# Two items' last k-times-v chunks in one 64x64 step of the array, and the pair stretch moved ahead of the second product

## The chip, the cores and the metric

The kernel runs on one core of a Trainium2 chip. The metric is device time in microseconds (us), lower is better, as the median of several executions. Engines: TensorE (PE, its weight loads PEld), VectorE (DVE), ScalarE (ACT), GpSimd (POOL), SyncE (SP, which issues most transfers).

## The reference

```python
def _attn_ref(q, k, v):               # (8, 8, 576, 64) each, float32
    q_s = softmax(q, axis=-1)         # written out: max, exp, sum + 1e-9, divide
    k_s = softmax(k, axis=2)          # over the 576 rows
    kv = np.einsum('bhsd,bhse->bhde', k_s, v)
    return np.einsum('bhsd,bhde->bhse', q_s, kv)

def _moe_ref(x, w_in, w_out):         # x: (4608, 512), 512 -> 2048 -> 512
    h = x @ w_in
    g = h * np.tanh(softplus(h))      # Mish
    return g @ w_out
```

The attention's output, heads side by side, is `x`.

## The kernel before

The 64 (batch, head) pairs are worked as 32 items of two heads each, four items to a block of 512 columns of x. Everything is float32; a matmul of plain float32 shows in the trace as two records, one for each of two passes. The MLP's factors are split into a high and a low part (`xs`, `wih`/`wil`, `gh`/`gl`, `wo`), three matmuls for each product.

The MLP runs in 144 slots (`NSLOT`). Slot n has a first product `h_mm(n)` (12 matmuls of 128x128 weights by 512 columns into one bank `ph`), Mish on ACT (`g_mish`, tile `y`), the split on DVE (`g_hi`, `g_lo`), and three slots later a second product `out_mm` (12 matmuls into four banks `po`). The order of the start is written out by hand in `FIRST`; after it `group(n)` takes four slots at a time, u = 0 to 3, with i = 4 + n/4 the number of the item whose attention is spread over that group. In a group, `m` is the slot of the first product and `o = m - 3` that of the second.

At u = 2 of every second group (i = 8, then i = 9, 11 to 31) stands `a_pair(e)`: for items e and e+1 the product of q and kv, namely `px` (512 columns, banks e and f) and `pt` (the last 64 columns), and for items f = e+2 and e+3 the product of k and v into `pkv` (`a_kv2`). Pair 6 (at i = 8) has only the k-times-v part, pair 30 only the px and pt part; pairs 8 to 28 have both.

k times v contracts the 576 rows in five chunks: four of 128 rows, and a last one of 64 real rows, with v's other 64 rows zero. Each chunk is two matmuls, one for each half of the output's partitions (128 rows by 64 columns of weights, `128*64` in the trace). px and pt use quarters of the array (`64*64`), four at a time.

After the matmuls, `a_tail2` (ACT) copies pt, `x_hi` (ACT) and `x_lo` (DVE) split px into `xs`, and `a_kvs2` (DVE) divides the k-times-v product by its sum into `kvt`, which the next pair's px and pt read. `pt`, `pkv` and the first product's `ph` share two banks g and h, taken in turn by `turn_bank`. At the end `evac` copies the last four `po` banks out; for the last of them ACT copies one half and DVE the other.

Of the kernel before, what the change touches and what calls it, by code (L numbers as in the profile page):

```python
# [9 lines left out]
F32 = mybir.dt.float32  # L10
F32R = mybir.dt.float32r
U32 = mybir.dt.uint32
AF = mybir.ActivationFunctionType
ALU = mybir.AluOpType
AX = mybir.AxisListType
P = 128
# [37 lines left out]
def attn_mish_mlp(ctx: ExitStack, tc: tile.TileContext, q, k, v, wu, qs, kt, v3, out):  # L54
# [32 lines left out]
    def bank(letter, name, dtype=F32):  # L87
        return ps.tile([P, 512], dtype, tag=f"bank_{letter}", name=name)
# [4 lines left out]
    def turn_bank(name):  # L93
        turn.append("gh"["gh".index(turn[-1]) ^ 1] if turn else "g")
        return bank(turn[-1], name)
# [78 lines left out]

    at = {}
    xs = {}
    ap.tile([P, 104], F32, tag="gap0", name="gap0")
    xt_dram = dp.tile([B, P, HP, ST], F32, name="xt_dram")


# [1 line left out]
    def v_tile(pool, tag, inner=False):  # L182
        if inner:
            t = pool.tile([P, D + 2, 2, NC + 1], F32, tag=tag, name=f"{tag}_0")
            ones, last = t[:, D:D + 2], t[ST:P, D:D + 2, :, NC]
        else:
            t = pool.tile([P, 2, NC + 1, D + 2], F32, tag=tag, name=f"{tag}_0")
            ones, last = t[:, :, :, D:D + 2], t[ST:P, :, NC, D:D + 2]
        nc.gpsimd.memset(ones, 1.0)
        nc.gpsimd.memset(last, 0.0)  # L190
        return t
# [36 lines left out]
    def v_load(i):  # L228
        if i >= NITEM:
            return  # L230
        t = at.setdefault(i, {})["v"] = pools["v"] if i > HP and i % 2 else vt[min(i, 3)]
        if i < 3:
            nc.sync.dma_start(t[:, 0:D], v3[i])
        else:
            nc.sync.dma_start(t[:, :, :, 0:D], v[i])

    def v_part(i, j, c):
        t = at[i]["v"]
        return t[:, :, j, c] if i < 3 else t[:, j, c]
# [170 lines left out]
    def a_x2(e, px, pt, order):  # L410
        for x, j, h in order:
            a, o = slice(h * D, (h + 1) * D), slice((h ^ j) * D, ((h ^ j) + 1) * D)
            nc.tensor.matmul((px, pt)[x][h][o], kvt[a, j], at[e + j]["qT"][x][a], start=True, stop=True)  # L413
        for j in range(2):
            at[e + j].update(dict(px=px[j]) if px else {}, **dict(pxt=pt[j]) if pt else {})
# [8 lines left out]
        fill(f"XP{e}", px[0])  # L424
        a_x2(e, px, None, [(0, j, h) for j in range(2) for h in range(2)])

    def a_xpair(e):
        r1, r2 = (turn_bank(f"pt{e}_{j}") for j in range(2))
        px = [bank("ef"[j], f"px{e + j}") for j in range(2)]
        a_x2(e, px, (r1[:, 0:ST], r2[:, 2 * (D + 2):2 * (D + 2) + ST]),  # L430
             [(x, j, h) for x in (1, 0) for j in range(2) for h in range(2)])
        return r2

    def a_kv2(e, pkv):
        for i in range(e, e + 2):
            f = slice((i - e) * (D + 2), (i - e + 1) * (D + 2))
            for c in range(NC + 1):
                for j in range(2):
                    nc.tensor.matmul(pkv[j * D:(j + 1) * D, f], at[i]["ke"][:, c, j], v_part(i, j, c),  # L439
                                     start=c == 0, stop=c == NC)  # L440
        at[e]["pkv"] = pkv[:, 0:2 * (D + 2)].rearrange("p (i f) -> p i f", i=2)

    def a_kvp(e, b):
        pkv = bank(b, f"pkv{e}")
        fill(f"KP{e}", pkv)
        a_kv2(e, pkv)

    def a_kvs2(e):
        pkv = at[e]["pkv"]
        rs = ap.tile([P, 2], F32, tag="rs0", name=f"rs{e}")  # L450
        nc.vector.tensor_scalar_add(rs, pkv[:, :, D], 1e-9)
        nc.vector.reciprocal(rs, rs)
        nc.vector.tensor_tensor(kvt, pkv[:, :, 0:D], rs.unsqueeze(2).to_broadcast([P, 2, D]), ALU.mult)

    def a_pair(e):

        f = e + 2
        r2 = a_xpair(e) if e >= COLS else turn_bank(f"pkv{f}")
        if f < NITEM:
            a_kv2(f, r2)  # L460
        if e >= COLS:
            a_tail2(e)
            a_tail3(e)
            for j in range(2):
                x_hi(e + j, at[e + j]["px"])
                x_lo(e + j, at[e + j]["px"])
            a_tail2(e + 1)
            a_tail3(e + 1)
        if f < NITEM:
            a_kvs2(f)  # L470

# [3 lines left out]
    def a_tail2(i):  # L475
        if i < COLS:
            if not xt_first:
                xt_first.append(xp.tile([P, 16, ST], F32, tag=f"wo{NF - 1}", name="xt_first"))
            xt = xt_first[0][:, i]
        else:  # L480
            xt = ap_odd[:, 1] if i % 2 else ap.tile([P, ST], F32, tag="xt", name=f"xt{i}")
        at[i]["xt"] = xt
        nc.scalar.copy(xt, at[i]["pxt"])

    def a_tail3(i):
        b, hp = divmod(i, HP)
        nc.sync.dma_start(xt_dram[b, :, hp, :], at[i]["xt"])
# [30 lines left out]
    def h_mm(n):  # L518
        for t in range(HP):
            h_part(n, t)  # L520
# [42 lines left out]
            nc.tensor.matmul(po[t], g[a][:, t * P:(t + 1) * P], wo[f][:, z], start=f == 0 and i == 0,  # L563
                             stop=f == NF - 1 and i == 2)

    def evac(c, t, *copies):
        ob = sp.tile([P, DM], F32, tag="wc", name=f"ob{c}_{t}")
        w = DM // len(copies)
        for j, copy in enumerate(copies):
            copy(ob[:, j * w:(j + 1) * w], po[t][:, j * w:(j + 1) * w])  # L570
        if c < COLS // HP:
            nc.sync.dma_start(out[c * S:c * S + SM, :].rearrange("(p c) e -> p c e", c=NC)[:, t, :], ob)
        elif c < B:
            nc.sync.dma_start(out[c * S + t * P:c * S + (t + 1) * P, :], ob)
        else:
            for j, eng in enumerate((nc.sync, nc.scalar)):
                e = (2 * t + j + 1) * S
                eng.dma_start(out[e - ST:e, :], ob[j * ST:(j + 1) * ST])

    def group(n):  # L580
        i = HP + n // G

        ka, kb = (i + 2, NITEM) if i % 2 else (COLS + 1 if i == COLS else NITEM, i + 2)
        for u in range(G):
            m, o = n + u, n + u - LAG
            if m < NSLOT:
                h_mm(m)
            if u == 0:
                if NITEM <= i < NITEM + HP:
                    t_load(i - NITEM)  # L590
                if i == COLS:
                    v_load(i + 1)
                a_qsum(i)
                if i < NITEM:
                    a_qmul(i)
            if u == 1:
                a_qt(i)
                a_ksub(ka)
            if 0 <= o < NSLOT:
                out_mm(o)  # L600
            if m < NSLOT:
                g_mish(m)
            if 0 <= o < NSLOT and o % NF == NF - 1:
                for t in range(NC):
                    evac(o // NF, t, nc.scalar.copy if t % 2 else nc.vector.tensor_copy)
            if m < NSLOT:
                g_hi(m)
                g_lo(m)
            if u == 0:
                a_kmx(ka)  # L610
                if ka < NITEM:
                    kt_load(ka + 1)
            if u == 1:
                a_exp(ka, "k")
                if ka < NITEM:
                    k_load(ka + 1)
                a_qm(i + 1)
            if u == 2:
                if i % 2 and COLS < i < NITEM:
                    a_pair(i - 1)  # L620
                    v_load(i + 3)
                    v_load(i + 4)
                elif i == COLS:
                    a_pair(i - 2)
                    v_load(i + 2)
                    v_load(i + 3)
                elif NITEM <= i < NITEM + HP:
                    x_hi(i, tails[i - NITEM])
                    x_lo(i, tails[i - NITEM])
                a_kmx(kb)  # L630
                if kb < NITEM:
                    kt_load(kb + 1)
            if u == 3:
                a_ksub(kb)
        a_exp(kb, "k")
        a_exp(i + 1, "q")
        if kb < NITEM:
            k_load(kb + 1)
        q_load(i + 2)
# [16 lines left out]
    with tc.manual_schedule(engines={ET.Activation, ET.PE, ET.DVE, ET.Pool, ET.SP}):  # L656
        for token in first:
            name, number, banks = re.fullmatch("([A-Z]+)([0-9]*)([a-h]*)", token).groups()
            stages[name](*([int(number)] if number else []), *([banks] if banks else []))
            if name == "H" and banks in ("g", "h"):  # L660
                turn[:] = [banks]
        for n in range(NF, NSLOT, G):
            group(n)

        for t in range(NC):
            for n in range(NSLOT - LAG, NSLOT):
                out_part(n, t)
            evac(B, t, nc.scalar.copy, *([nc.vector.tensor_copy] if t == NC - 1 else []))


# [43 lines left out]
```

## Time and profile before

| | |
|---|---|
| median of 3 runs | 867.15 us (867.15 to 868.44) |
| profiled execution, its own time | 867.23 us |
| its span, first to last instruction | 865.4 us (1.83 us lie around it) |
| mean granted TensorE clock | 0.998 |
| PE busy | 850.8 us (98%) |
| DVE, ACT, POOL busy | 459.1, 327.9, 142.5 us |

PE is busy nearly throughout and its granted clock is full, so the time is the number of PE instructions by their spacing, plus what is lost between unlike ones. Start times of successive matmuls say more than the busy time, since the records overlap.

### The profile page before, as it was taken

To read this page: it belongs to the slowest core of one execution; us is meant where nothing else is said; L and a number is where in the kernel's file an instruction comes from. 1 tells how busy PE (TensorE), PEld (TensorE's weight loads), DVE (VectorE), ACT (ScalarE), POOL (GpSimd) and SP (SyncE) were. 2 spreads that over 40 slices of the span, in tenths; PEclk is the share of its full clock that TensorE was granted. 3 is DMA by queue.
4 is the path that set the end of the run, shared out by engine and by line. 5 is a ranking of instruction groups with operands and counts; after the bars stand their busy time and mean duration, and the time that the engine had idled before them with its cause. 6 is when DMAs were issued, how large, how long until landed. Compare 5 with 4: busy or idle time off the path is not lost.

```text
span 865.4 us, 11716 instructions
## 1 busy us (share of the span) xinstructions
PE 850.8 (98%) x4468; PEld 689.5 (80%) x4468; DVE 459.1 (53%) x1207; ACT 327.9 (38%) x485; POOL 142.5 (16%) x128
## 2 busy tenths in 40 slices
PE   7899999999999999999999999999999999999997
PEld 6677878787878888787878787878788788888886
DVE  6888876646574647464655656564743222222221
ACT  4889854424342434333342334243422111111111
POOL 8996520011111110011111011111110000000000
PEclk9999999999999999999999999999999999999999
DMA  9975335203222223212231313122100020001001
GB/s 332 357 290 144 113 86 151 66 25 83 80 65 46 73 48 120 49 57 63 91 77 44 77 63 91 29 62 83 54 16 0 16 73 13 0 1 49 1 0 49
DMA packets 69944, 67.87 MB, mean 78 GB/s; under 512 B 49024, under 2 KB 49024, under 8 KB 69888
## 3 DMA queue, kind: packets, MB, share of 16 engines
q1 hardware_dynamic: 69568, 66.60, 26.0%
q8 instruction: 35, 0.57, 0.3%
q10 hardware_dynamic: 320, 0.52, 0.2%
q14 instruction: 21, 0.17, 0.1%
HBM read 56.62 MB, written 10.49 MB: 78 GB/s over the span
## 4 chain that ended last, share of the span: by engine, by line
PE 91%; ACT 2%; DVE 2%; POOL 2%; DMA 2%; issue 1%; POOLq 0%; ACTq 0%; DVEq 0%; SPq 0%
PE ph L515 43%; PE po L563 43%; PE pt L439 2%; PE px L413 1%; DMA raw_out<-in_w_dram 1%; PE pkv L439 1%; POOL kt L313 1%; ACT wa L131 0%; PE pt L413 0%; POOL q L370 0%; DMA q<-in_q_dram 0%; ACT ph L534 0%; ACT L534 0%; POOL q L112 0%; DMA xt_dram<-xt_first 0%
## 5 line engine op out<-in xcount | busy, mean ns | idle before, releaser
L515 PE MATMUL ph<-xs,wih 128*128 128x512 f32 x1152 | 358.4, 392 | 1.1 <-DVE gl L112 1.1
L563 PE MATMUL po<-wo,gh 128*128 128x512 f32 x1152 | 355.2, 389 | 1.2 <-POOL wo L112 1.2
L563 PEld LDWEIGHTS po<-wo,gh 128*128 128x128 f32 x1152 | 216.1, 188 | 47.2 <-POOL wo L112 1.6
L515 PEld LDWEIGHTS ph<-xs,wih 128*128 128x128 f32 x1152 | 213.7, 188 | 49.4 <-issue 1.6
L515 PE MATMUL ph<-xs,wil 128*128 128x512 f32 x576 | 224.6, 390 | 0.0
L563 PE MATMUL po<-wo,gl 128*128 128x512 f32 x576 | 224.1, 389 | 0.0
L538 ACT ACTIVATE y<-ph 128x512 f32<-128x512 f32 x128 | 76.7, 599 | 373.5 <-PE ph L515 314.0
L543 DVE CAST gh<-y 128x512 fp32r<-128x512 f32 x128 | 57.4, 449 | 271.5 <-ACT y L538 271.3
L515 PEld LDWEIGHTS ph<-xs,wil 128*128 128x128 f32 x576 | 108.1, 188 | 23.4 <-POOL wil L112 0.4
L563 PEld LDWEIGHTS po<-wo,gl 128*128 128x128 f32 x576 | 108.1, 188 | 22.6
L112 DVE TENSOR_TENSOR gl<-y,gh 128x512 fp32r<-128x512 f32 x128 | 88.6, 692 | 11.9
L370 POOL TENSOR_TENSOR qe<-qe,qs 128x576 f32<-128x576 f32 x24 | 27.9, 1163 | 296.5 <-DVE qs L366 296.5
L538 ACT ACT_TABLE_LOAD x35 | 44.9, 1283 | 71.3 <-PE ph L515 71.3
L112 POOL TENSOR_TENSOR q<-q,qm 128x576 f32<-128x576 f32 (+1 forms) x32 | 38.1, 1193 | 197.8 <-DVE qm L267 186.6
L347 ACT ACT_TABLE_LOAD x43 | 55.2, 1283 | 6.1 <-DMA q<-in_q_dram 3.7
L570 DVE COPY ob<-po 128x512 f32<-128x512 f32 (+1 forms) x17 | 11.5, 676 | 38.5 <-PE po L563 29.1
L356 DVE TENSOR_REDUCE qs<-qe 128x18 f32<-128x576 f32 x24 | 18.1, 752 | 25.2 <-ACT qe L347 25.2
L495 DVE TENSOR_TENSOR xs<-px,xs 128x512 fp32r<-128x512 f32 x32 | 20.7, 685 | 17.0 <-ACT xs L492 16.8
L276 DVE TENSOR_REDUCE qm<-q 128x18 f32<-128x576 f32 (+1 forms) x32 | 24.4, 762 | 4.3 <-DMA q<-in_q_dram 4.2
L246 DVE TENSOR_REDUCE mxd<-kt 128x1 f32<-128x576 f32 x32 | 23.8, 745 | 1.5 <-DMA kt<-in_kt_dram 1.5
L252 DVE STREAM_TRANSPOSE mb<-mxd 32x32 f32<-32x32 f32 x96 | 19.5, 203 | 3.1
L492 ACT CAST xs<-px 128x512 fp32r<-128x512 f32 x32 | 17.4, 591 | 7.4 <-PE px L413 7.4
(115 smaller groups left out, 566.5 us busy)
## 6 DMA issues: line engine op xcount, KB each, us to landing
kt<-in_kt_dram SPq DMA_DIRECT2D x32, 288.0 KB, 2.9
k<-in_k_dram SPq DMA_DIRECT2D x27, 320.0 KB, 3.0
raw_in<-in_w_dram SPq DMA_DIRECT2D x16, 512.0 KB, 7.9
raw_out<-in_w_dram SPq DMA_DIRECT2D x16, 512.0 KB, 5.6
out_dram<-ob SPq DMA_DIRECT2D x32, 256.0 KB, 2.2
q<-in_qs_dram SPq DMA_DIRECT2D x24, 288.0 KB, 3.0
v<-in_v_dram SPq DMA_DIRECT2D x18, 320.0 KB, 3.8
v_odd<-in_v_dram SPq DMA_DIRECT2D x14, 320.0 KB, 4.6
```

Source lines behind the costliest of these rows:

```text
L112: eng.tensor_tensor(out, a, b, ALU.subtract)
L246: nc.vector.tensor_reduce(mxd, r["kt"], axis=AX.X, op=ALU.max)
L252: nc.vector.transpose(mb[h, h], mxd[h].to_broadcast([32, 32]))
L276: nc.vector.tensor_reduce(qm, qt, axis=AX.X, op=ALU.max)
L347: nc.scalar.activation(e, r[nm], AF.Exp)
L370: eng.tensor_tensor(q2, q2, z.unsqueeze(2).to_broadcast(list(q2.shape)), ALU.mult)
L439: nc.tensor.matmul(pkv[j * D:(j + 1) * D, f], at[i]["ke"][:, c, j], v_part(i, j, c), start=c == 0, stop=c == NC)
L495: nc.vector.tensor_tensor(xs[i][:, 1], src, xs[i][:, 0].bitcast(F32), ALU.subtract)
L515: nc.tensor.matmul(gs[n], wi[a][:, t, fs], x[:, z], start=t == 0 and i == 0, stop=t == HP - 1 and i == 2)
L538: nc.scalar.activation(y, gs[n], AF.Mish)
L543: copy(hi, gs[n])
L563: nc.tensor.matmul(po[t], g[a][:, t * P:(t + 1) * P], wo[f][:, z], start=f == 0 and i == 0, stop=f == NF - 1 and i == 2)
```

## The change

In a pair the order on PE becomes: px, pt, four chunks of item f, four chunks of item f+1, and then the two last chunks together as four matmuls of 64 rows by 64 columns, each on a quarter of the array: item f in rows 0 to 63, item f+1 in rows 64 to 127. For that the host rolls the tail rows of v of items 5, 7, ... by 64 and `v_tile` clears the other half of `v_odd`. The two items of a pair write to two banks, each shared with one of the pt tiles: `r[0]` and `r[1]` instead of `r2` alone.

The whole pair (PE, ACT and DVE parts) now stands between `h_mm(m)` and `out_mm(o)` of u = 2, with `g_mish(m)` ahead of it, and so `g_hi(m)` and `g_lo(m)` behind it. At u = 1 of those groups a Mish of one column (`early`) is added behind the exp of k. `a_kvs2` reads two banks (five DVE instructions in place of three). The last `evac` is one copy on ACT.

```diff
-            ones, last = t[:, :, :, D:D + 2], t[ST:P, :, NC, D:D + 2]
+            ones = t[:, :, :, D:D + 2]
+            last = t[0:ST, :, NC, D:D + 2] if tag == "v_odd" else t[ST:P, :, NC, D:D + 2]
...
-    def a_xpair(e):
-        r1, r2 = (turn_bank(f"pt{e}_{j}") for j in range(2))
-        px = [bank("ef"[j], f"px{e + j}") for j in range(2)]
-        a_x2(e, px, (r1[:, 0:ST], r2[:, 2 * (D + 2):2 * (D + 2) + ST]),
-             [(x, j, h) for x in (1, 0) for j in range(2) for h in range(2)])
-        return r2
...
+    def a_kvi(pkv, i, last=NC + 1):
+        for c in range(last):
+            for j in range(2):
+                nc.tensor.matmul(pkv[j * D:(j + 1) * D], at[i]["ke"][:, c, j], v_part(i, j, c),
+                                 start=c == 0, stop=c == NC)
...
+        for i in range(2):
+            nc.vector.tensor_scalar_add(rs[:, i:i + 1], pkv[i][:, D:D + 1], 1e-9)
         nc.vector.reciprocal(rs, rs)
-        nc.vector.tensor_tensor(kvt, pkv[:, :, 0:D], rs.unsqueeze(2).to_broadcast([P, 2, D]), ALU.mult)
+        for i in range(2):
+            nc.vector.tensor_tensor(kvt[:, i], pkv[i][:, 0:D], rs[:, i:i + 1].to_broadcast([P, D]), ALU.mult)
 
     def a_pair(e):
 
+
+
         f = e + 2
-        r2 = a_xpair(e) if e >= COLS else turn_bank(f"pkv{f}")
+        px = [bank("ef"[j], f"px{e + j}") for j in range(2)] if e >= COLS else None
+        if px:
+            a_x2(e, px, None, [(0, j, h) for j in range(2) for h in range(2)])
+        r = [turn_bank(f"pt{e}_{j}") for j in range(2)]
+        pkv = [r[j][:, ST:ST + D + 2] for j in range(2)]
+        if px:
+            a_x2(e, None, [t[:, 0:ST] for t in r], [(1, j, h) for j in range(2) for h in range(2)])
         if f < NITEM:
-            a_kv2(f, r2)
-        if e >= COLS:
-            a_tail2(e)
-            a_tail3(e)
+            for j in range(2):
+                a_kvi(pkv[j], f + j, NC)
+            for j in range(2):
+                for i in range(2):
+                    a = slice(i * D, (i + 1) * D)
+                    nc.tensor.matmul(pkv[i][j * D:(j + 1) * D], at[f + i]["ke"][a, NC, j], at[f + i]["v"][a, j, NC],
+                                     start=False, stop=True)
+            at[f]["pkv"] = pkv
+        if px:
             for j in range(2):
                 x_hi(e + j, at[e + j]["px"])
                 x_lo(e + j, at[e + j]["px"])
-            a_tail2(e + 1)
-            a_tail3(e + 1)
+            for j in range(2):
+                a_tail2(e + j)
+                a_tail3(e + j)
...
+        pair = i - 1 if i % 2 and COLS < i < NITEM else COLS - 2 if i == COLS else None
         for u in range(G):
             m, o = n + u, n + u - LAG
             if m < NSLOT:
                 h_mm(m)
+            if u == 2 and pair is not None:
+                g_mish(m)
+                a_pair(pair)
...
             if u == 1:
                 a_exp(ka, "k")
+                if pair is not None:
+
+                    nc.scalar.activation(early, ident[:, 0:1], AF.Mish)
...
-            evac(B, t, nc.scalar.copy, *([nc.vector.tensor_copy] if t == NC - 1 else []))
+            evac(B, t, nc.scalar.copy)
...
+        if not fill:
+            tail[HP + 1::2] = _np.roll(tail[HP + 1::2], 64, axis=1)
```

On PE, pair 18 stood before the change like this, from the last matmuls of the second product to the first of the next first product (`x10` is ten matmuls, five chunks of two):

```order
L563 MATMUL po_3_3261<-wo_1259,gl_3671 128x512
L413 MATMUL pt_0_3818<-qTt_3566,kvt 64x64
L413 MATMUL pt_1_3819<-qTt_3566,kvt 64x64
L413 MATMUL pt_0_3818<-odd,kvt 64x64
L413 MATMUL pt_1_3819<-odd,kvt 64x64
L413 MATMUL px_3820<-qT_3565,kvt 64x512
L413 MATMUL px_3821<-qT_3565,kvt 64x512
L413 MATMUL px_3820<-qT_3753,kvt 64x512
L413 MATMUL px_3821<-qT_3753,kvt 64x512
L439 MATMUL pt_1_3819<-v_0_99,ke_3674 64x66 x10
L439 MATMUL pt_1_3819<-v_odd_420,ke_odd 64x66 x10
L515 MATMUL ph_3867<-xs_2658,wih 128x512 x2
```

After the change the same pair stands behind the first product and ahead of the second (line numbers are those of the changed kernel):

```order
L530 MATMUL ph_3808<-xs_3050,wil 128x512
L415 MATMUL px_3823<-qT_3585,kvt 64x512
...
L415 MATMUL px_3824<-qT_3773,kvt 64x512
L415 MATMUL pt_0_3829<-qTt_3586,kvt 64x64
...
L415 MATMUL pt_1_3830<-odd,kvt 64x64
L432 MATMUL pt_0_3829<-v_0_100,ke_3694 64x66 x8
L432 MATMUL pt_1_3830<-v_odd_421,ke_odd 64x66 x8
L474 MATMUL pt_0_3829<-v_0_100,ke_3694 64x66
L474 MATMUL pt_1_3830<-v_odd_421,ke_odd 64x66
L474 MATMUL pt_0_3829<-v_0_100,ke_3694 64x66
L474 MATMUL pt_1_3830<-v_odd_421,ke_odd 64x66
L578 MATMUL po_0_3275<-wo_1260,gh_3689 128x512 x2
```

Four of the twenty k-times-v matmuls become four quarter-array matmuls, and px now comes ahead of pt.

On ACT, around pair 16, the order before was:

```order
L347 ACT_TABLE_LOAD
L347 ACTIVATE ke_odd<-k_3285 128x640
L538 ACT_TABLE_LOAD
L538 ACTIVATE y_3419<-ph_3394 128x512
L483 COPY xt_3457<-pt_0_3425 128x64
L492 CAST xs_3460<-px_3427 128x512
L492 CAST xs_3463<-px_3428 128x512
L483 COPY odd<-pt_1_3426 128x64
L538 ACTIVATE y_3499<-ph_3474 128x512
```

And it is now:

```order
L349 ACT_TABLE_LOAD
L349 ACTIVATE ke_odd<-k_3302 128x640
L634 ACT_TABLE_LOAD
L634 ACTIVATE early<-ident 128x1
L553 ACTIVATE y_3425<-ph_3412 128x512
L507 CAST xs_3459<-px_3427 128x512
L507 CAST xs_3462<-px_3428 128x512
L498 COPY xt_3465<-pt_0_3433 128x64
L498 COPY odd<-pt_1_3434 128x64
L553 ACTIVATE y_3519<-ph_3494 128x512
```

The table load that belonged to Mish of slot m now belongs to `early`, ahead of it; the number of table loads on ACT is the same, and the orders of SP and POOL are unchanged.

## Rows read from the trace of the kernel before

**Rows 1.** The page: busy time by engine, and granted clock in 40 slices.
```profile
PE 850.8 (98%) x4468; PEld 689.5 (80%) x4468; DVE 459.1 (53%) x1207; ACT 327.9 (38%) x485; POOL 142.5 (16%) x128
...
PEclk9999999999999999999999999999999999999999
```

**Rows 2.** The chain that ended last, in order of time: start us, us, what.
```profile
397.14 2.96 PE ph L515 x12
...
443.36 2.96 PE ph L515 x12
```

**Rows 3.** Timeline of PE, pair 18: start, us, then the instruction with its count.
```profile
394.30 0.39 PE L563 MATMUL po<-wo,gl 128*128 128x512 f32 x1
394.62 0.27 PE L413 MATMUL pt<-qTt,kvt 64*64 64x64 f32 x2
...
394.78 1.04 PE L413 MATMUL px<-qT,kvt 64*64 64x512 f32 x8
395.75 0.81 PE L439 MATMUL pt<-v,ke 128*64 128x66 f32 x20
396.39 0.75 PE L439 MATMUL pt<-v_odd,ke_odd 128*64 128x66 f32 x20
397.07 0.73 PE L515 MATMUL ph<-xs,wih 128*128 128x512 f32 x2
```

**Rows 4.** Line 439 and line 413, all runs: ns min/median/max, first and last start.
```profile
L439 PE MATMUL pt<-v_odd,ke_odd x220: 219/222/223, 165.3 to 628.0; 128*64 128x66 f32 x110
L413 PE MATMUL px<-qT,kvt x128: 589/590/640, 18.0 to 672.6; 64*64 64x512 f32 x128
```

**Rows 5.** Timeline of PE in the start: a pt step by itself between first products.
```profile
113.75 0.40 PE L515 MATMUL ph<-xs,wil 128*128 128x512 f32 x1
114.07 0.27 PE L413 MATMUL pt<-qTt,kvt 64*64 64x64 f32 x2
...
114.35 0.73 PE L515 MATMUL ph<-xs,wih 128*128 128x512 f32 x2
```

**Rows 6.** Timeline at the end of a first product: its last matmul, and Mish.
```profile
386.14 0.39 PE L515 MATMUL ph<-xs,wil 128*128 128x512 f32 x1
...
386.62 0.60 ACT L538 ACTIVATE y<-ph 128x512 f32<-128x512 f32 x1 [3.56 <-PE ph L515]
```

**Rows 7.** Timeline in the start: PE released by ACT.
```profile
17.18 0.57 ACT L404 COPY qT<-pq 128x512 f32<-128x512 f32 x1
...
17.81 0.37 PE L413 MATMUL pt<-qT,kvt 64*64 64x64 f32 x3 [0.32 <-ACT qT L404]
```

**Rows 8.** Timeline of ACT and DVE around pair 18.
```profile
388.79 0.74 ACT L347 ACTIVATE ke_odd<-k 128x640 f32<-128x640 f32 x1 [0.26 <-DVE k L334]
392.05 1.28 ACT L538 ACT_TABLE_LOAD   x1 [2.52 <-PE ph L515]
...
395.87 1.08 ACT L492 CAST xs<-px 128x512 fp32r<-128x512 f32 x2 [0.60 <-PE px L413]
...
396.49 1.29 DVE L495 TENSOR_TENSOR xs<-px,xs 128x512 fp32r<-128x512 f32 x2 [1.29 <-ACT xs L492]
...
398.08 0.29 DVE L453 TENSOR_TENSOR kvt<-pt,rs 128x128 f32<-128x128 f32 x1
```

**Rows 9.** Timeline at pair 6: last matmul of the first product, and Mish.
```profile
137.15 0.39 PE L515 MATMUL ph<-xs,wil 128*128 128x512 f32 x1
...
137.58 0.60 ACT L538 ACTIVATE y<-ph 128x512 f32<-128x512 f32 x1 [1.49 <-PE ph L515]
```

**Rows 10.** Timeline at the end of the span.
```profile
859.05 0.59 ACT L570 COPY ob<-po 128x512 f32<-128x512 f32 x1 [1.45 <-PE po L563]
...
861.09 0.37 ACT L570 COPY ob<-po 128x256 f32<-128x256 f32 x1 [1.45 <-PE po L563]
...
861.49 0.42 DVE L570 COPY ob<-po 128x256 f32<-128x256 f32 x1 [9.38 <-ACT ob L570]
861.95 0.47 SPq L578 DMA_DIRECT2D out_dram<-ob  x1
```

More of the change, by code (lines that the diff above doesn't have):

```diff
@@ L176, in attn_mish_mlp @@
     xs = {}
-    ap.tile([P, 104], F32, tag="gap0", name="gap0")
+    ap.tile([P, 96], F32, tag="gap0", name="gap0")
+    early = ap.tile([P, 1], F32, tag="early", name="early")
     xt_dram = dp.tile([B, P, HP, ST], F32, name="xt_dram")
@@ L425, in a_xp @@
         a_x2(e, px, None, [(0, j, h) for j in range(2) for h in range(2)])
-    def a_xpair(e):
-        r1, r2 = (turn_bank(f"pt{e}_{j}") for j in range(2))
-        px = [bank("ef"[j], f"px{e + j}") for j in range(2)]
-        a_x2(e, px, (r1[:, 0:ST], r2[:, 2 * (D + 2):2 * (D + 2) + ST]),
-             [(x, j, h) for x in (1, 0) for j in range(2) for h in range(2)])
-        return r2
[L434 to L441, printed above, removed]
+    def a_kvi(pkv, i, last=NC + 1):
[3 more added lines that the diff above has]
+                                 start=c == 0, stop=c == NC)
     def a_kvp(e, b):
@@ L445, in a_kvp @@
         fill(f"KP{e}", pkv)
-        a_kv2(e, pkv)
+        for i in range(2):
+            a_kvi(pkv[:, i * (D + 2):(i + 1) * (D + 2)], e + i)
+        at[e]["pkv"] = pkv[:, 0:2 * (D + 2)].rearrange("p (i f) -> p i f", i=2)
     def a_kvs2(e):
@@ L450, in a_kvs2 @@
         rs = ap.tile([P, 2], F32, tag="rs0", name=f"rs{e}")
-        nc.vector.tensor_scalar_add(rs, pkv[:, :, D], 1e-9)
+        if e < COLS:
+            nc.vector.tensor_scalar_add(rs, pkv[:, :, D], 1e-9)
+            nc.vector.reciprocal(rs, rs)
+            nc.vector.tensor_tensor(kvt, pkv[:, :, 0:D], rs.unsqueeze(2).to_broadcast([P, 2, D]), ALU.mult)
+            return
+        for i in range(2):
+            nc.vector.tensor_scalar_add(rs[:, i:i + 1], pkv[i][:, D:D + 1], 1e-9)
         nc.vector.reciprocal(rs, rs)
-        nc.vector.tensor_tensor(kvt, pkv[:, :, 0:D], rs.unsqueeze(2).to_broadcast([P, 2, D]), ALU.mult)
+        for i in range(2):
+            nc.vector.tensor_tensor(kvt[:, i], pkv[i][:, 0:D], rs[:, i:i + 1].to_broadcast([P, D]), ALU.mult)
     def a_pair(e):
         f = e + 2
-        r2 = a_xpair(e) if e >= COLS else turn_bank(f"pkv{f}")
-        if f < NITEM:
-            a_kv2(f, r2)
-        if e >= COLS:
-            a_tail2(e)
-            a_tail3(e)
+        px = [bank("ef"[j], f"px{e + j}") for j in range(2)] if e >= COLS else None
[5 more added lines that the diff above has]
+            a_x2(e, None, [t[:, 0:ST] for t in r], [(1, j, h) for j in range(2) for h in range(2)])
+        if f < NITEM:
+            for j in range(2):
+                a_kvi(pkv[j], f + j, NC)
+            for j in range(2):
+                for i in range(2):
+                    a = slice(i * D, (i + 1) * D)
[3 more added lines that the diff above has]
+        if px:
             for j in range(2):
@@ L564, in out_part, with evac @@
                              stop=f == NF - 1 and i == 2)
-    def evac(c, t, *copies):
+    def evac(c, t, copy):
         ob = sp.tile([P, DM], F32, tag="wc", name=f"ob{c}_{t}")
-        w = DM // len(copies)
-        for j, copy in enumerate(copies):
-            copy(ob[:, j * w:(j + 1) * w], po[t][:, j * w:(j + 1) * w])
+        copy(ob, po[t])
         if c < COLS // HP:
@@ L600, in group @@
                 out_mm(o)
-            if m < NSLOT:
+            if m < NSLOT and not (u == 2 and pair is not None):
                 g_mish(m)
@@ L618, in group @@
             if u == 2:
[L619 to L626, printed above, removed]
+                if pair is not None:
+                    v_load(pair + 4)
+                    v_load(pair + 5)
                 elif NITEM <= i < NITEM + HP:
@@ L680 @@
     DM, DFF = w_in.shape
+    HP = 4
     N, SM = B * H // 2, S // 128 * 128
```

## Prediction

> **What bounds the kernel now.** I read the page first. PE is busy 98% of the span at a full granted clock, and DVE, ACT and POOL have 47% of the span or more to spare [rows 1]. Such a busy share alone says little, because the records of successive matmuls overlap. So I read the chain of waits in order of time: in the steady part it is PE all the way, one first product behind each pair, 46.22 us from pair to pair (397.14 to 443.36) [rows 2]. The 192 main matmuls of such a period (eight first and eight second products of 12) are the same in both kernels. What the change can move is the stretch of a pair, from the last main matmul ahead of it to the first one behind it.
>
> The timeline of PE gives that stretch for pair 18 [rows 3]; the other full pairs look alike. The reader is to look at starts, not at durations. The last matmul of the second product starts at 394.30, and a main matmul holds the array about 0.227 us (a product of 12 fills 2.72 us). The next could start at 394.53, but pt starts at 394.62. So 0.09 us go by empty when PE passes from whole-array matmuls to quarters. No releaser stands in that row: it is not a wait for another engine.
>
> The k-times-v part is 40 records, in 20 steps of two (two halves of the array at once). Item 19's first record starts at 396.39 and its last ends 0.75 us later; a record lasts 0.222 us [rows 3, 4], so its last step starts at 396.92. Nine steps took 0.53 us: **0.059 us a step**. From that last step to the first product it is 0.15 us (396.92 to 397.07): the step's own 0.059 and again 0.09 of empty array.
>
> **The change part by part.**
>
> *The shared last chunk.* Removed are four steps (two items, one chunk each, two passes): 4 x 0.059 = 0.236 us. Added is one group of four quarter matmuls in two passes. Its nearest relative is pt: four quarter matmuls of 64 columns, where the new ones have 66. In the start of the kernel one pt group stands alone between two first products, and takes 0.28 us from its first start to the next first product (114.07 to 114.35), with its exposed weight load and its passage to the whole array in it [rows 5]. Ahead of it PE passes from halves to quarters. No row shows that passage. The passages that rows do show are whole to quarters (0.09, above), halves to whole (0.09, above) and quarters to halves: px's last record starts at 395.23 (394.78 + 1.04 - 0.59), a pass of px holds the array 0.43 us (those 0.45 less some 0.02 between the four starts), and k times v comes 0.52 us later, at 395.75: 0.09 again [rows 3, 4]. I bound the unseen passage by 0 and 0.09 and take 0.09, the value of both neighbours.
>
> From the sixteenth step on, before: 4 x 0.059 + 0.15 = 0.386 us to the next main matmul. After: 0.15 to the quarter group and 0.28 from there = 0.43 us. So the shared step costs **+0.044 us** a pair; with no passage it would be 0.059 + 0.059 + 0.15 = 0.268 us, **-0.118 us**. Twelve pairs have it (6 to 28): +0.53 us, or -1.42 us at the other bound.
>
> The Trainium skill ("TensorEngine Tiling (Array Packing)", Tiling Modes, Key Properties) says that a change of tiling mode, and not only of tile, drains TensorE. It speaks against this change: by it the new group pays a passage of its own and the twelve pairs come out at +0.53 us, without it at -1.42 us. The 0.09 us at the passages of [rows 3] agree with it; no run here yet shows halves to quarters.
>
> *px ahead of pt.* Before, pt and px together take from 394.62 to 395.75 [rows 3], with one exposed weight load (0.05 us, the 640 against 590 ns of a px record [rows 4]) at whichever comes first. The order within does not change the sum: 0.
>
> *The new place.* The stretch is entered from a first product in place of a second, and left into a second in place of a first; both are whole-array matmuls of the same spacing, so this costs 0, as long as nothing is waited for. Two waits have to be covered.
>
> First, `r[1]` is the bank that the first product of slot m just filled. pt's second matmul and all later PE work stand behind the wait for Mish of slot m. Call the start of the first product's last matmul T. Mish starts at T + 0.48 and ends at T + 1.08 (386.14, then 386.62 and 0.60) [rows 6]; PE starts 0.06 us after ACT's end (17.18 + 0.57 to 17.81) [rows 7], and its weight load takes 0.05: T + 1.19. PE gets to pt at T + 0.32 (as 113.75 to 114.07 [rows 5]), + 0.05 for the exposed load of px, + 0.88 for px (394.78 to 395.75, less the 0.09 of passage): T + 1.25. **Covered by 0.06 us.** That is thin, and the bounds are 0 and what Mish is late.
>
> This holds only if no table load stands ahead of Mish. Before, one did: 1.28 us, started when the first product was done [rows 8]. `early` takes it: it comes behind the exp of k, which ends at 389.53, so the table is loaded by 390.81, and a one-column activation, shorter than the 0.60 us of a full Mish [rows 6], is done by 391.4, ahead of 392.05, where the load started before [rows 8].
>
> Second, the next first product writes `r[0]`, which ACT's pt copies and DVE's `a_kvs2` must have read. Px copies start about 0.1 us after px. Shifted to the new place, DVE's two x_lo (0.6 us behind the first ACT copy, 1.29 us) end some 2 us after px. Five small DVE instructions follow: three took 0.59 us (397.78 to 398.37) [rows 8], so five take about 1.0. Together that is about T + 4.3. PE needs T + 0.32 + 1.13 + 20 steps less four (0.94) + 0.43 + 2.72 = T + 5.5. Covered by over 1 us; if the second product were not there, about 1.5 us would be lost each pair. `gh` and `gl` of slot m come behind it on DVE, about 2.5 us later than before, and are read three slots later, some 16 us.
>
> *Pair 6* has no px to cover Mish. k times v enters at T + 0.32 = 137.47 and reaches the second bank after 0.05 + 8 x 0.059 us, at 137.99. Mish ends at 138.18 [rows 9], and with 0.11 for wake-up and load PE goes on at 138.29: **+0.30 us**, once.
>
> *The last evac.* The halves did not run side by side: ACT 861.09 to 861.46, DVE 861.49 to 861.91, transfer at 861.95. One ACT copy took 0.59 us for the chunk before [rows 10]: 861.68, transfer 0.04 later at 861.72. **-0.23 us**, on the path.
>
> The sum: 0.53 + 0.30 - 0.23 = +0.60 us. The profiled execution took 867.23 us, 0.08 above the median of the runs shown. The forecast is 867.8 us.
>
> **The rivals.** *The passage costs nothing* (halves and quarters share their columns, so the array need not empty). For it: pt to px, both quarters, shows no empty time [rows 3]. Against it: every change of form seen costs 0.09. Then -1.42 + 0.30 - 0.23 = -1.35: 865.9 us.
>
> *Mish is late for `r[1]`.* The slower side: PE stands at pt's second matmul in the twelve pairs with px. The place decides when the 0.06 us of cover are gone; each 0.1 us beyond costs 1.2 us. For it: the cover is thin, and is built from records at rest. Against it: the wake-up and the length of Mish are steady. At 0.1 us late it is 869.0 us.
>
> *`early` does not bring the table in ahead.* Then Mish ends 1.28 us later, and PE waits 1.28 - 0.06 = 1.22 us in twelve pairs: +14.6 us, 882 us. The order on ACT speaks against it, as it stands there ahead of the load's former place.
>
> **How the numbers follow.** A measurement of this kernel can tell about 0.2% from no change, 1.73 us: faster is below 865.4, slower above 868.9. The forecast has a chance of 0.53, and by itself a range of 867.0 to 868.6 (the small terms off by half). The free passage has 0.24; it lies just inside the bound, and I give a third of it to the faster side. Late Mish has 0.18, two thirds of it slower. The table load has 0.02, slower. 0.03 are left for gains that I don't see. Faster: 0.08 + 0.03 = 0.11; slower: 0.12 + 0.02 = 0.14; the same: 0.75. The range runs from the free passage with a little beyond, 865.4, to Mish 0.1 us late with a little beyond, 869.2; it leaves out about 0.18.
>
> **What the profile after would show.** Right: behind the last of 16 steps of a pair the group of line 474 starts 0.15 us later, and the second product 0.28 us after that; PE has no idle time put down to Mish at pt, but about 0.3 us at pair 6; the period of 46.22 us becomes 46.26; the last transfer leaves 0.23 us earlier after the last matmul. A step of 0.06 us to line 474 would show the free passage. A start of pt's second matmul later than the first by more than 0.05 us would show Mish late, and a table load behind the first product the last rival. The forecast is wrong if the quarter group does not run four at a time like pt, since each further pass adds 0.06 us in twelve pairs.

## The result and the profile after

| | before | after |
|---|---|---|
| median of 22 runs each | 867.13 us (866.32 to 868.45) | 868.41 us (867.38 to 869.27) |
| profiled execution, its span | 867.23, 865.4 us | 868.05, 866.2 us |

The ratio is 1.0014 with a 95% interval of 1.0008 to 1.0021: a loss of 1.3 us, 0.7 to 1.8 us by the interval. That lies within the 0.2% that the prediction called no change, in its range of 865.4 to 869.2 us, and on the side it forecast (867.8 us). The sum behind it (+0.60 us) was too small by about half, and one pair is the reason.

Stretches and periods below are taken from the unrounded starts, so the difference of two printed starts can be off by 0.01 us. T is, as in the prediction, the start of the last matmul of the first product of slot m.

The timeline of PE at pair 18, with the row of Mish on ACT, answers to [rows 3]. (L530 and L578 are the two products, L415 px and pt, L432 the whole chunks, L474 the shared step.)

```profile
392.42 0.39 PE L530 MATMUL ph<-xs,wil 128*128 128x512 f32 x1
...
392.74 1.09 PE L415 MATMUL px<-qT,kvt 64*64 64x512 f32 x8
392.91 0.60 ACT L553 ACTIVATE y<-ph 128x512 f32<-128x512 f32 x1 [1.02 <-PE ph L530]
...
393.56 0.13 PEld L415 LDWEIGHTS pt<-qTt,kvt 64*64 64x64 f32 x1 [0.20 <-ACT y L553]
...
393.65 0.22 PE L415 MATMUL pt<-qTt,kvt 64*64 64x64 f32 x2
...
393.88 0.69 PE L432 MATMUL pt<-v,ke 128*64 128x66 f32 x16
394.39 0.64 PE L432 MATMUL pt<-v_odd,ke_odd 128*64 128x66 f32 x16
394.96 0.27 PE L474 MATMUL pt<-v,ke 64*64 64x66 f32 x1
...
395.09 0.22 PE L474 MATMUL pt<-v_odd,ke_odd 64*64 64x66 f32 x1
...
395.24 0.73 PE L578 MATMUL po<-wo,gh 128*128 128x512 f32 x2
```

The last whole step starts at 394.39 + 0.64 - 0.22 = 394.81, the shared step 0.15 us behind it, and the second product 0.28 us behind that (394.96 to 395.24). These are the two numbers that the prediction put there. The stretch, from the last main matmul ahead (392.42) to the first behind, is 2.81 us; before it was 2.77 (394.30 to 397.07 [rows 3]). pt's matmuls go through without a wait: Mish ends at 393.51, and the weight load that waited for it starts at 393.56, ahead of pt's first matmul at 393.65. All ten pairs from 10 to 28 have this stretch.

The chain of waits answers to [rows 2]: the product behind a pair now starts 46.24 us after that of the pair before (395.31 to 441.55), against 46.22.

```profile
395.31 2.95 PE po L578 x12
441.55 2.95 PE po L578 x12
```

Pair 8, the first of the pairs with px, is another matter. The timeline of PE there:

```profile
160.46 0.39 PE L530 MATMUL ph<-xs,wil 128*128 128x512 f32 x1
160.78 1.09 PE L415 MATMUL px<-qT,kvt 64*64 64x512 f32 x8
161.69 0.27 PE L415 MATMUL pt<-qTt,kvt 64*64 64x64 f32 x2
162.37 0.27 PE L415 MATMUL pt<-qTt,kvt 64*64 64x64 f32 x1 [0.41 <-ACT y L553]
...
164.00 0.74 PE L578 MATMUL po<-wo,gh 128*128 128x512 f32 x2
```

Its stretch is 3.54 us, 0.7 more than pair 18's. pt's second matmul starts 0.68 us after its first and names Mish (`y`) as its releaser. ACT's timeline shows why Mish is late, first in the kernel after, then, for the table load of the exp, in the kernel before:

```profile
158.28 1.28 ACT L349 ACT_TABLE_LOAD   x1 [2.18 <-DVE k L336]
159.57 0.74 ACT L349 ACTIVATE ke_odd<-k 128x640 f32<-128x640 f32 x1
160.33 1.28 ACT L634 ACT_TABLE_LOAD   x1
161.62 0.20 ACT L634 ACTIVATE early<-ident 128x1 f32<-128x1 f32 x1
161.73 0.58 ACT L553 ACTIVATE y<-ph 128x512 f32<-128x512 f32 x1
```

```profile
157.73 1.28 ACT L347 ACT_TABLE_LOAD   x1 [1.61 <-DVE k L334]
```

The table load of the exp stands idle until DVE has subtracted the maximum from k; only then come the exp, the second load and `early`. At pair 18 the first load did not wait; the exp alone waited for DVE, 0.26 us [rows 8]. So it is at all the pairs 10 to 28, in both kernels: the load starts 4.3 us ahead of T, right behind the Mish before it, where at pair 8 it starts 2.2 us ahead (2.75 in the kernel before). Why the load itself is held at pair 8 alone, no run here shows.

Pair 6, on PE, shows the 0.3 us that was forecast (its stretch is 1.97 us, 136.82 to 138.79; before it was 1.64, from 139.87 to 141.51 in the old place):

```profile
136.82 0.39 PE L530 MATMUL ph<-xs,wil 128*128 128x512 f32 x1
137.14 0.69 PE L432 MATMUL pt<-v,ke 128*64 128x66 f32 x16
137.90 0.69 PE L432 MATMUL pt<-v_odd,ke_odd 128*64 128x66 f32 x16
...
138.79 0.73 PE L578 MATMUL po<-wo,gh 128*128 128x512 f32 x2
```

The end of the span answers to [rows 10]. The last matmul starts at 861.64, and the last transfer leaves 1.04 us later; before it was 860.66 and 1.29 us.

```profile
861.64 0.39 PE L578 MATMUL po<-wo,gl 128*128 128x512 f32 x1
862.07 0.59 ACT L583 COPY ob<-po 128x512 f32<-128x512 f32 x1 [1.45 <-PE po L578]
862.68 0.50 ACTq L591 DMA_DIRECT2D out_dram<-ob  x1
```

Added up: ten pairs (10 to 28) at 0.02, pair 6 at 0.33, pair 8 at 3.54 - 2.77 = 0.77, the end at -0.25: +1.05 us, within the interval of the measured loss. The traces agree with this sum: from T of pair 6 to the end of the span it is 728.3 us before (from 137.15) and 729.4 after (from 136.82).

### The profile page after: what moved, and what is told of

Its sections match the earlier page's. It is cut to its first block, busy times and chain, and to the rows that moved or that the text cites. A ratio compares the mean times of both kernels' runs of the same rounds, so it can differ in the third digit from the quotient of the medians.

```text
span 866.2 us, 11763 instructions
## 1 busy us (share of the span) xinstructions
PE 851.4 (98%) x4468; PEld 692.3 (80%) x4468; DVE 460.2 (53%) x1230; ACT 329.4 (38%) x498; POOL 142.5 (16%) x128
## 4 chain that ended last, share of the span: by engine, by line
PE 88%; ACT 3%; DVE 3%; POOL 2%; DMA 2%; issue 1%; SPq 0%; DVEq 0%; ACTq 0%; POOLq 0%
PE po L578 42%; PE ph L530 41%; PE px L415 2%; PE pt L432 1%; DMA raw_out<-in_w_dram 1%; DMA q<-in_q_dram 1%; PE pkv L432 1%; ACT wa L131 1%; POOL q L372 0%; POOL raw_in L139 0%; POOL kt L315 0%; DVE gl L112 0%; PE pt L474 0%; DVE gh L558 0%; POOL wil L112 0%
## 5 line engine op out<-in xcount | busy, mean ns | idle before, releaser
L578 PE MATMUL po<-wo,gh 128*128 128x512 f32 x1152 | 356.8, 391 | 1.2 <-POOL wo L112 1.2
L530 PE MATMUL ph<-xs,wih 128*128 128x512 f32 x1152 | 356.7, 391 | 1.1 <-DVE gl L112 1.1
L530 PEld LDWEIGHTS ph<-xs,wih 128*128 128x128 f32 x1152 | 214.7, 188 | 48.6 <-issue 1.6
L578 PEld LDWEIGHTS po<-wo,gh 128*128 128x128 f32 x1152 | 215.1, 188 | 47.5 <-POOL wo L112 1.6
L530 PE MATMUL ph<-xs,wil 128*128 128x512 f32 x576 | 224.4, 390 | 0.0
L578 PE MATMUL po<-wo,gl 128*128 128x512 f32 x576 | 224.3, 389 | 0.0
L530 PEld LDWEIGHTS ph<-xs,wil 128*128 128x128 f32 x576 | 108.1, 188 | 22.9 <-POOL wil L112 0.3
L578 PEld LDWEIGHTS po<-wo,gl 128*128 128x128 f32 x576 | 108.1, 188 | 22.6
L583 DVE COPY ob<-po 128x512 f32<-128x512 f32 x16 | 11.1, 692 | 26.8 <-PE po L578 26.8
L583 ACT COPY ob<-po 128x512 f32<-128x512 f32 x20 | 11.8, 589 | 22.3 <-PE po L578 22.3
```

The lines of the kernel that those rows point to most:

```text
L530: nc.tensor.matmul(gs[n], wi[a][:, t, fs], x[:, z], start=t == 0 and i == 0, stop=t == HP - 1 and i == 2)
L583: copy(ob, po[t])
```

## The experiments

Each is the changed kernel with one edit, except e7 (the kernel before with one), e8 (three edits) and e9 (the place of pair 6 and its banks). Medians stand beside those of the kernel before, run in turn with them on the same chip (867.20 us for e1 to e4, 867.24 for e5 to e8, 867.30 for e9). Medians of 11 runs leave about 0.8 us open either way (e3 and e4, with effects of over 12 us, have two runs each), so the small terms are read from the trace. The start of the kernel adds to that: the last main matmul ahead of pair 6 starts at 136.82 us in one trace and at 137.51 in another of the same code up to there.

**e1: five whole chunks again, in the new place.**

```diff
-                a_kvi(pkv[j], f + j, NC)
-            for j in range(2):
-                for i in range(2):
...
+                a_kvi(pkv[j], f + j)
```

> The changed kernel with the shared last chunk undone: both items keep five whole 128-row chunks, in their own banks and in the new place. Theory (the shared step saves four steps of 0.059 us but pays a passage of the array of 0.09 us and an exposed weight load, so it is a small loss): the stretch of a pair goes from 2.813 to 2.77 us, 12 pairs, about 0.5 us less in all than the changed kernel; pairs 6 and 8 keep their waits of about 0.3 and 0.7 us. Rival (the shared step gains, and the loss is in the new place or the two banks alone): the stretch gets longer, by about 0.1 us a pair, 1.4 us more in all.

867.87 us, ratio 1.0008 (1.0000 to 1.0017). PE at pair 18:

```profile
392.66 0.39 PE L525 MATMUL ph<-xs,wil 128*128 128x512 f32 x1
...
394.75 0.76 PE L432 MATMUL pt<-v_odd,ke_odd 128*64 128x66 f32 x20
395.43 0.73 PE L573 MATMUL po<-wo,gh 128*128 128x512 f32 x2
```

The stretch is 2.77 us, as in the kernel before. So the new place and the two banks cost nothing in a steady pair, and the 0.04 us that a steady pair loses is the shared step. Pair 8 still waits (stretch 3.49 us, 160.82 to 164.32). A small miss: pair 6 does not keep its wait of 0.3 us. Its stretch is 1.81 us (137.33 to 139.14), 0.17 more than in the kernel before, where nothing waits, because the two further steps of the first item cover more of Mish.

**e2: the shared step right behind pt, ahead of the whole chunks.**

```diff
-                a_kvi(pkv[j], f + j, NC)
-            for j in range(2):
...
-                                     start=False, stop=True)
+                                     start=True, stop=False)
+            for i in range(2):
+                for c in range(NC):
+                    for j in range(2):
+                        nc.tensor.matmul(pkv[i][j * D:(j + 1) * D], at[f + i]["ke"][:, c, j], v_part(f + i, j, c),
+                                         start=False, stop=c == NC - 1)
```

> The changed kernel with the shared quarter step moved: right behind pt, which uses quarters too, and ahead of the four whole chunks of both items. The work is the same, only one passage of the array fewer in the eleven pairs 8 to 28. Theory (the passage eats the gain): the stretch falls from 2.813 to about 2.65 us, 11 x 0.16 = 1.8 us less than the changed kernel, some 0.5 us less than the kernel before. Rival (the quarter step itself is slow, or the order does not matter): the stretch stays at about 2.81 us and the time that of the changed kernel.

866.89 us, ratio 0.9999 (0.9990 to 1.0008), 1.5 us less than the changed kernel's median. PE at pair 18:

```profile
392.41 0.39 PE L533 MATMUL ph<-xs,wil 128*128 128x512 f32 x1
...
393.71 0.22 PE L415 MATMUL pt<-odd,kvt 64*64 64x64 f32 x2
393.76 0.22 PE L472 MATMUL pt<-v,ke 64*64 64x66 f32 x1
...
393.84 0.22 PE L472 MATMUL pt<-v_odd,ke_odd 64*64 64x66 f32 x1
393.98 0.69 PE L477 MATMUL pt<-v,ke 128*64 128x66 f32 x16
...
395.07 0.73 PE L581 MATMUL po<-wo,gh 128*128 128x512 f32 x2
```

Behind pt the same step follows at 0.05 us, and all eight records start within 0.08 us (393.76 to 393.84). The stretch is 2.66 us, 0.16 less than in the changed kernel. The step is fast; the passage into it from whole chunks is what cost. A miss: pair 6 got worse, 2.43 us against 1.97. There the quarter group comes first and writes both banks, so PE stands at its second matmul from the start and the chunks of the first item no longer cover any of Mish:

```profile
137.51 0.33 PE L472 MATMUL pt<-v,ke 64*64 64x66 f32 x2
138.27 0.27 PE L472 MATMUL pt<-v_odd,ke_odd 64*64 64x66 f32 x1 [0.43 <-ACT y L556]
```

**e3: no one-column Mish.**

```diff
-                    nc.scalar.activation(early, ident[:, 0:1], AF.Mish)
```

> The changed kernel without the one-column Mish at u = 1. Theory (Mish of slot m is covered by px by some 0.06 us, and a table load of 1.28 us ahead of it comes through but for that): PE waits about 1.22 us at pt's second matmul in pairs 10 to 28, about 0.5 us more than now in pair 8, nothing more in pairs 6 and 30, in all 12 to 13 us more than the changed kernel, near 881 us. Rival (the load is hidden anyway): no change.

880.98 us, ratio 1.0160 (1.0141 to 1.0179), 12.6 us above the changed kernel. PE and ACT at pair 18:

```profile
399.67 0.27 PE L415 MATMUL pt<-qTt,kvt 64*64 64x64 f32 x2
400.86 0.27 PE L415 MATMUL pt<-qTt,kvt 64*64 64x64 f32 x1 [0.91 <-ACT y L553]
...
398.92 1.28 ACT L553 ACT_TABLE_LOAD   x1 [2.52 <-PE ph L530]
```

The stretch is 4.04 us (398.45 to 402.49), 1.23 more than with `early`, in all the pairs from 8 to 28. Of a load of 1.28 us, about 0.05 us were covered; the prediction had worked out 0.06.

**e4: the pair back behind the second product, shared step and two banks kept.**

```diff
-            if u == 2 and pair is not None:
-                g_mish(m)
-                a_pair(pair)
...
                 if pair is not None:
+                    a_pair(pair)
                     v_load(pair + 4)
```

> The changed kernel with the pair back in its old place, behind the second product and the split of slot m; the shared step and the two banks stay. Theory (the next first product needs the bank r[0], which the k-times-v scaling on DVE and the copy of pt on ACT must have read; ahead of the second product that is covered, here it is not): PE waits about 1.2 us behind each pair, 13 to 15 us more than the changed kernel, near 882 us, while the waits for Mish in pairs 6 and 8 are gone. Rival (the new place brings nothing): the time of the changed kernel less about 1 us.

884.21 us, ratio 1.0197 (1.0179 to 1.0216), 15.8 us above the changed kernel, a little more than expected. The table of waits of PE, and the matmul that waits behind pair 18:

```profile
PE ph L530 <- DVE kvt L454: 14.7, 12, 1.4
...
405.95 0.70 PE L530 MATMUL ph<-xs,wih 128*128 128x512 f32 x2 [1.24 <-DVE kvt L454]
```

The stretch is 4.13 us, 1.3 more than in the new place. With two shared banks the new place is needed: it hides the scaling on DVE behind the second product.

**e5: at item 9, k's subtraction ahead of q's transposes on DVE.**

```diff
             if u == 1:
+                if i == COLS + 1:
+                    a_ksub(ka)
                 a_qt(i)
-                a_ksub(ka)
+                if i != COLS + 1:
+                    a_ksub(ka)
```

> The changed kernel, where for item 9 alone DVE subtracts the maximum from k of item 11 ahead of the transposes of q, not behind them. Theory (pair 8's wait of about 0.7 us comes from DVE: the subtraction is late, ACT's table load for the exp waits for it, then the exp, the second table load, the one-column Mish and Mish of slot m follow one behind the other): the exp starts about 0.8 us earlier, the wait at pair 8 falls from about 0.7 to under 0.1 us, and the time is about 0.7 us less than the changed kernel's. Rival (the load of the table or Mish itself is slow there): the wait stays.

867.59 us, ratio 1.0005 (0.9997 to 1.0014). ACT and PE at pair 8:

```profile
158.24 1.28 ACT L349 ACT_TABLE_LOAD   x1 [1.46 <-DVE k L336]
...
161.15 0.39 PE L530 MATMUL ph<-xs,wil 128*128 128x512 f32 x1
...
163.96 0.73 PE L578 MATMUL po<-wo,gh 128*128 128x512 f32 x2
```

The load waits 1.46 us in place of 2.18, and the stretch of pair 8 is 2.82 us, within 0.01 us of the others. The wait was the chain that begins with DVE's subtraction.

**e6: pair 6 in banks e and f.**

```diff
-        r = [turn_bank(f"pt{e}_{j}") for j in range(2)]
+        r = [turn_bank(f"pt{e}_{j}") if px else bank("ef"[j], f"pt{e}_{j}") for j in range(2)]
```

> The changed kernel, where pair 6, which has no px, puts its two k-times-v products into banks e and f, which are free then, and not into the bank that Mish of slot m still reads. Theory (pair 6 waits 0.3 us for Mish): its stretch falls from 1.97 to about 1.68 us, 0.3 us less in all; pair 8 keeps its wait, or loses part of it, if DVE's work behind pair 6 then comes earlier. Rival (the wait has another cause): no change.

868.34 us, ratio 1.0013 (1.0004 to 1.0022): the median can't tell 0.3 us. The trace can; pair 6's stretch is 1.68 us:

```profile
137.10 0.39 PE L530 MATMUL ph<-xs,wil 128*128 128x512 f32 x1
...
138.78 0.73 PE L578 MATMUL po<-wo,gh 128*128 128x512 f32 x2
```

Pair 8 keeps its wait (3.53 us, 160.45 to 163.97): it does not come from pair 6's own wait.

**e7: the kernel before with one copy on ACT at the end.**

```diff
-            evac(B, t, nc.scalar.copy, *([nc.vector.tensor_copy] if t == NC - 1 else []))
+            evac(B, t, nc.scalar.copy)
```

> The kernel before with the last part of the change alone: the last bank is copied out by ACT in one piece. Theory (the two halves run one behind the other): the last transfer leaves 1.05 us behind the start of the last matmul in place of 1.29 us, 0.24 us less in all. Rival (the halves overlap, or the end of the transfer is set elsewhere): no change or a loss of 0.2 us.

866.98 us, ratio 0.9998 (0.9989 to 1.0007): no verdict from the time. In the trace the last transfer leaves 1.04 us after the last matmul's start, against 1.29:

```profile
860.89 0.39 PE L563 MATMUL po<-wo,gl 128*128 128x512 f32 x1
...
861.93 0.50 ACTq L578 DMA_DIRECT2D out_dram<-ob  x1
```

**e8: the edits of e2, e5 and e6 together.**

> The changed kernel with the shared quarter step behind pt, the subtraction for item 11 ahead of the transposes, and pair 6 in banks e and f. Theory: the three gains add, 1.8 + 0.7 + 0.3 = 2.8 us less than the changed kernel and 1.5 us less than the kernel before. Rival (the waits are of one cause and are counted twice, or a new wait comes in): at most 1.8 us less than the changed kernel.

865.72 us, ratio 0.9983 (0.9974 to 0.9992): 1.5 us under the kernel before and 2.7 us under the changed one. It is the version that beats both. The stretch of pair 18 is 2.66 us (391.25 to 393.90), that of pair 6 1.68 and that of pair 8 2.66; no PE wait for Mish is left.

**e9: pair 6 alone in its old place, in banks e and f.**

```diff
-        r = [turn_bank(f"pt{e}_{j}") for j in range(2)]
+        r = [turn_bank(f"pt{e}_{j}") if px else bank("ef"[j], f"pt{e}_{j}") for j in range(2)]
...
-            if u == 2 and pair is not None:
+            if u == 2 and pair is not None and i > COLS:
...
                 if pair is not None:
+                    if i == COLS:
+                        a_pair(pair)
                     v_load(pair + 4)
```

> The changed kernel, where pair 6 alone stays in its old place behind the second product, the copies out and the split of slot m, with its products in banks e and f so that nothing waits for them. Theory (two things make pair 8 late: the table load that waits for the subtraction on DVE, which costs about 0.25 us there whatever pair 6 does, and some 0.5 us by which DVE's work falls back because pair 6 now stands ahead of the second product of slot 15, whose copies out DVE must make first): the wait at pair 8 falls from 0.73 to about 0.25 us, pair 6 takes about 1.68 us, and the time is 0.7 to 0.8 us less than the changed kernel's. Rival (pair 6's place has no part in it): the wait at pair 8 stays at 0.7 us, and only 0.3 us are gained.

867.20 us, ratio 0.9998 (0.9989 to 1.0007), 1.2 us less than the changed kernel's median where 0.7 to 0.8 were expected; the traces give 0.84 (0.55 at pair 8, 0.29 at pair 6). Pair 8's stretch is 2.99 us, of which 0.17 is wait, against 0.73 in the changed kernel:

```profile
161.50 0.39 PE L530 MATMUL ph<-xs,wil 128*128 128x512 f32 x1
...
164.49 0.74 PE L578 MATMUL po<-wo,gh 128*128 128x512 f32 x2
```

So about 0.17 us of pair 8's wait lies in the load chain as such, and about 0.55 us comes with the move of pair 6 (its banks alone, in e6, left the wait as it was).

## Why the prediction was right, and where its sum was off

*The shared last chunk*: right, by its own steps. The unseen passage from halves to quarters was taken at 0.09 us between bounds of 0 and 0.09; both starts came out as put there, and the stretch grew by 0.04. e1 took the loss away by undoing the step alone, e2 turned it into a gain of 0.12 us against before by moving the step to where the array was in quarters already. The free-passage rival is out. The period grew by only 0.02 us, where 0.04 were forecast, since the 12 main matmuls behind the stretch went by in 2.85 us (395.24 to 398.09) in place of 2.87 (397.07 to 399.94): 0.2 us over ten pairs in place of 0.44. In e1 the period is 46.22 us again, so this 0.02 us comes with the shared step; why, the runs leave open.

*The cover of Mish by px*: right for the ten pairs 10 to 28 and for its size; e3 measured 0.05 for the 0.06 us.

*The cover of* `r[0]`: right. DVE's scaling at pair 18 ends at 396.54 us, and the next first product starts at 398.09. In e4, without this cover, a pair took 1.3 us longer, where the prediction put about 1.5.

*Wrong was the step that priced all full pairs by pair 18* ("the other full pairs look alike", and from there "the table is loaded by 390.81"). On PE they do look alike, 2.77 us each; on ACT pair 8 does not. At pair 8 the exp's load itself waits for DVE, and the trace of before showed it: it starts at 157.73, so load, exp, load and `early` end at 161.2, where Mish would start at 160.95. That is 0.2 to 0.3 us, less the 0.06 of cover, and e9 found 0.17. The other 0.55 us came with the move. With pair 6 ahead of it the second product of slot 15 ends later, and DVE's copies out of it push the rest of DVE's work back; POOL's multiplication for item 9 then starts at 151.53 in place of 150.85, and lies across the cast of `gh`, which takes 0.99 us in place of 0.43. First the kernel after, then the one before:

```profile
151.97 0.99 DVE L558 CAST gh<-y 128x512 fp32r<-128x512 f32 x1 [0.59 <-ACT y L553]
...
151.53 1.16 POOL L372 TENSOR_TENSOR qe<-qe,qs 128x576 f32<-128x576 f32 x1 [14.64 <-DVE qs L368]
```

```profile
150.85 1.17 POOL L370 TENSOR_TENSOR qe<-qe,qs 128x576 f32<-128x576 f32 x1 [13.64 <-DVE qs L366]
...
151.99 0.43 DVE L543 CAST gh<-y 128x512 fp32r<-128x512 f32 x1 [1.29 <-ACT y L538]
```

DVE's subtraction for item 11 comes 0.55 us later by that (157.42 in place of 156.87), and the chain up to pair 8 with it. e9 shows that pair 6's place decides about 0.55 us; that the cast is the link is read from the traces and was not tried by itself. The other runs speak for it: in e9, where POOL's multiplication (152.02 to 153.18) meets the cast (from 153.02) for under 0.2 us, the cast takes 0.45 us, and in e1, e2, e3, e5, e6 and e8, with pair 6 in the new place, 0.99. The trace of before holds the same long cast ahead of pairs 12, 16, 20, 24 and 28 (0.98 to 0.99 us, the first at 244.43). There DVE's subtraction ends 2.26 us ahead of T, where at pairs 10, 14, 18 and 26 it is 2.82, and PE does not wait, because the table load has run ahead of it. Only at pair 8, where the load waits for the subtraction, does the delay reach PE.

That the sum came as near as it did is in part luck: the ten pairs were put 0.24 us too high and pair 8 0.73 too low, and the two errors partly cancel.

*Late Mish*, a rival with a chance of 0.18 that was priced for all twelve pairs, thus came in one pair, at 0.73 us. *Pair 6* and *the last evac* came out at 0.33 (0.04 of it the shared step's own cost) and -0.25 for 0.30 and -0.23. At pair 6 the shared step also takes cover from Mish: in e1, without it, 0.16 of the 0.33 us are gone. *The new place* costs 0 in a steady pair (e1) and is needed with the two shared banks (e4).

## What to carry to other kernels

Count the passages between tile shapes of the array before packing small matmuls: here each change of shape left it empty for about 0.09 us and exposed a weight load, so a packed step is a gain beside work of the same shape and a loss in between. When a stretch of work is moved, look at the first and the last of its instances, not only at a steady one; a cover of 0.06 us holds where everything repeats and fails at the edge. With a loss of 0.1%, starts in the trace say more than medians.

## What was not expected of the hardware

The DVE cast of 128x512 that takes 0.43 us took 0.99 us where POOL's 1.16 us multiplication lay across it, ending 0.27 us after POOL's; where the two met for under 0.2 us, this cast took 0.43 to 0.45. And four quarter matmuls in two passes behind another quarter group start all their eight records within 0.08 us, where the same group behind a passage takes 0.13 us (394.96 to 395.09).
